# Gated attention/MLP mix: gate row turned by a matmul, b1 taken along in a projection unit, b2 loaded last, fusion chunks and attention sums regrouped

## Chip, cores, metric

One core of a Trainium2 chip. The metric is the device time of one execution in microseconds.

Names: PE is the matmul engine and PEld its weight loads, DVE the vector engine, ACT the scalar engine, POOL the GpSimd engine, SP the engine whose queue issues most DMAs. PSUM is the memory that PE writes to; a pair is two of its banks, and a unit can start only when its pair is free. A cast is a copy out of PSUM that also makes bf16 of it. K0, V2, Q1 and so on are units of the projections to keys, values and queries, numbered by pairs of token tiles. kv are the sums over the tokens, nm the numerators and den the denominators of the attention, hp the units of the first MLP layer.

## The reference, cut

```python
g = sigmoid((x * gate_w).sum(-1, keepdims=True))
a = A_ref(x, wqkv, w_phi, wo)      # linear attention, softmax feature maps, 16 heads of 28
b = gelu(x @ w1 + b1) @ w2 + b2    # F = 1792
return g * a + (1 - g) * b         # x: 2048 tokens of 448, bf16
```

The kernel fuses `wk @ w_phi` and `wq @ w_phi` on the chip first ("the fusions"). The gate sum `x @ gate_w` takes one more column: the gate row, turned to a column, is stored as column 448 of the fused weights, so that some projections are 449 wide and deliver it.

## The kernel before

The parts that the change and the argument touch:

```python
gb = consts.tile([32, P], BF16, name="gb")          # rows: 14 of b1, 4 of the gate
gbT = consts.tile([P, 32], BF16, name="gbT")        # the same, turned
...
nc.gpsimd.dma_start(gb[16:19, :], gate_w[0:384]...)
nc.gpsimd.dma_start(gb[19:20, :]..., gate_w[384:448]...)
nc.gpsimd.dma_start(gb[0:NJ, :], B_b1.rearrange("(j p) -> j p", p=P))
...
nc.gpsimd.dma_start(b2b[:], B_b2[None, :].to_broadcast([P, D]))   # about 11.4 us
load_wT(WkT, D)                       # turned loads, all on SP, in this order
load_wT(WqT, 0)
load_x(512, 512)
nc.sync.dma_start_transpose(gbT[:], gb[:])          # the gate turn
load_x(1024, 512)
...
def prep(W_T, W_out, s, copies):      # a fusion: chunks 2, 3, then 0, 1
    for h in (1, 0):
        w_ps = pair("w_ps", slot=(s + 1 - h) % 4)
        for i in range(2):
            c = 2 * h + i
            ... 4 matmuls ...
        copies[1 - h](out=W_out[:, 2*h:2*h+2, 0:D], in_=w_ps[:, :, 0:D])
...
twin(WkT)                             # ACT copy that chunk 3 of the fusion needs
prep(WkT, Wpk, 1, (nc.scalar.copy, nc.vector.tensor_copy))        # first fusion
...
prep(WqT, Wpq, 3, (nc.vector.tensor_copy, nc.vector.tensor_copy)) # second fusion
nc.vector.tensor_copy(out=Wpq[:, :, D], in_=gbT[:, 16:20])
nc.vector.tensor_copy(out=WvG[:, :, D], in_=gbT[:, 16:20])
nc.vector.tensor_copy(out=b1T[:], in_=gbT[:, 0:NJ])
...
visit([(K, 1), (V, 2)], [(Q, 0)], 0, 2)   # V2: first reader of the gate column of WvG
...
kv_half(0); kv_half(1)                # sums over the tokens, four head pairs each
... nm matmuls of four tiles, num_out (DVE) of four tiles, then hp units (w1) go on
```

The softmax here doesn't subtract the row's maximum and nothing guards it: scores larger than these inputs give would overflow.

## Time and profile before

| | |
|---|---|
| time | 152.51 us (median of 4) |
| span of the profiled run | 150.3 us |
| PE busy | 144.6 us, 96% |
| DVE, ACT, POOL busy | 54, 43, 49% |
| first matmul of the first fusion | 9.13 us |
| V2 begins | 16.03 us |
| first hp unit / first kv matmul | 43.44 / 61.57 us |
| last DVE operation begins | 147.22 us |

In the chain of waits and in the timelines a row is: start in us, duration in us, engine, source line, operation, output<-inputs; a bracket says how long the engine was idle before it and what ended that. A group of pipelined matmuls ("x6") is shown longer than the distance to the next one, because the ends are modelled; distances are taken from starts. Source lines shift between the kernels: w_ps is L315 before and L319 after, full projections are L204 and L203.

### The profile page before, as it was taken

The numbers are of one execution on the slowest core, as the hardware profiler recorded it, in microseconds if no ns is written. First come the engines' busy times: TensorE is split into PE (matmuls) and PEld (weight loads), VectorE is DVE, ScalarE is ACT, GpSimd is POOL, SyncE is SP. The second block draws the span as 40 slices with busy tenths as digits, with TensorE's granted clock in tenths as the row PEclk, the third lists the DMA queues.
The fourth block names the chain that finished last, engine by engine and source line by source line (L and its number), as shares of the span: only waits on it lengthen the run. The fifth ranks groups of instructions, "written<-read, shape, count | busy, mean of one in ns | idle before, by whom it ended". The sixth has DMA issues, their size and how long they took to land.

```text
span 150.3 us, 3083 instructions
## 1 busy us (share of the span) xinstructions
PE 144.6 (96%) x1281; PEld 74.2 (49%) x1281; DVE 81.7 (54%) x139; ACT 63.9 (43%) x71; POOL 73.4 (49%) x60
## 2 busy tenths in 40 slices
PE   7989799999999999999999999999999999999991
PEld 2445344555544444774444445554455555545561
DVE  0248488999969992049995000740637847044112
ACT  3346277989999876506767674000000000000000
POOL 7992127799996999900399960000611110024000
PEclk9999999999999999999999999999999999999999
DMA  4997969679999959994629991140302423303201
GB/s 88 290 196 120 209 153 191 136 170 220 218 219 231 361 126 138 212 120 96 74 41 173 173 139 36 37 100 10 122 31 65 100 70 70 70 2 120 65 31 31
DMA packets 46334, 18.99 MB, mean 126 GB/s; under 512 B 36784, under 2 KB 46128, under 8 KB 46320
## 3 DMA queue, kind: packets, MB, share of 16 engines
q1 hardware_dynamic: 45568, 18.18, 58.3%
q10 hardware_dynamic: 544, 0.37, 0.9%
q0 software_dynamic: 208, 0.23, 0.9%
q8 instruction: 10, 0.16, 0.5%
q14 instruction: 4, 0.03, 0.1%
HBM read 6.34 MB, written 1.84 MB: 54 GB/s over the span
## 4 chain that ended last, share of the span: by engine, by line
PE 88%; DMA 7%; SPq 1%; DVE 1%; issue 0%
PE hp L431 28%; PE y L526 28%; PE y L204 6%; PE q_ps L234 5%; DMA gel<-in_A_wqkv_dram 4%; PE k_ps L234 4%; DMA gbT<-gb 3%; PE v_ps L234 3%; PE nm L455 3%; PE kv L443 2%; PE v_ps L204 2%; PE q_ps L204 2%; PE k_ps L204 2%; PE y L214 1%; PE w_ps L315 1%; SPq L116 1%
## 5 line engine op out<-in xcount | busy, mean ns | idle before, releaser
L526 PE MATMUL y<-w_sb,gel 128*128 128x448 bf16 (+1 forms) x224 | 43.8, 350 | 0.0
L431 PE MATMUL hp<-xT,w_sb 64*128 64x512 bf16 x224 | 42.8, 376 | 0.0
L431 PE MATMUL hp<-xS,w_sb 64*128 64x512 bf16 x168 | 40.7, 376 | 0.0
L435 ACT ACTIVATE gel<-hp,b1T 128x1024 bf16<-128x1024 f32 x28 | 30.8, 1113 | 14.6 <-PE hp L431 14.2
L526 PEld LDWEIGHTS <-gel 128*128 128x128 bf16 x238 | 22.3, 98 | 19.3 <-issue 0.4
L431 PEld LDWEIGHTS <-w_sb 64*128 64x128 bf16 x392 | 18.9, 94 | 23.2 <-DVE o_all L468 0.5
L491 POOL TENSOR_SCALAR b2u<-b2b,ungate 128x448 f32<-128x448 bf16 x16 | 10.0, 637 | 40.5 <-DVE res L538 40.5
L261 POOL TENSOR_TENSOR gel<-gel,rec 128x1792 bf16<-128x1792 bf16 x8 | 25.6, 3212 | 7.1 <-DVE lg L270 4.8
L538 DVE SCALAR_TENSOR_TENSOR res<-y,ungate,b2u 128x448 bf16<-128x448 f32 (+1 forms) x16 | 10.3, 673 | 25.0 <-PE y L526 13.2
L261 POOL TENSOR_TENSOR phiq<-phiq,rec 128x1792 bf16<-128x1792 bf16 x4 | 12.7, 3211 | 9.6 <-DVE rec L260 9.6
L252 ACT ACTIVATE gel<-k_ps 128x896 bf16<-128x896 f32 x16 | 13.7, 922 | 6.5 <-PE k_ps L214 4.9
L258 DVE TENSOR_REDUCE sums<-gel 128x64 f32<-128x1792 bf16 x8 | 16.0, 1996 | 0.0
L462 DVE TENSOR_SCALAR den<-nm,enL 128x16 f32<-128x16 f32 x16 | 3.6, 228 | 17.2 <-PE nm L455 17.2
L261 POOL TENSOR_TENSOR phqT<-phqT,rec 128x1792 bf16<-128x1792 bf16 x4 | 12.7, 3213 | 0.0
L468 DVE TENSOR_TENSOR o_all<-nm,den 128x448 bf16<-128x448 f32 (+2 forms) x24 | 11.0, 485 | 0.6
L234 PEld LDWEIGHTS <-xT 64*128 64x128 bf16 x104 | 8.6, 94 | 4.8
L204 PEld LDWEIGHTS <-xT 128*128 128x128 bf16 x66 | 5.9, 98 | 8.1 <-issue 2.8
L280 DVE CAST vaug<-v_ps 128x896 bf16<-128x896 f32 x7 | 7.5, 1072 | 4.3 <-PE v_ps L214 2.9
L260 DVE RECIPROCAL rec<-sums 128x64 f32<-128x64 f32 x16 | 8.9, 553 | 1.1
L234 PEld LDWEIGHTS <-xS 64*128 64x128 bf16 x78 | 7.3, 94 | 3.6
L234 PE MATMUL q_ps<-gel,xT 64*128 64x448 bf16 x48 | 8.6, 349 | 0.0
L204 PE MATMUL y<-wo_sb,phiq 128*128 128x448 bf16 (+1 forms) x36 | 8.2, 349 | 0.0
(88 smaller groups left out, 149.5 us busy)
## 6 DMA issues: line engine op xcount, KB each, us to landing
w_sb<-in_B_w_dram SPq DMA_DIRECT2D x4, 784.0 KB, 12.3
out_dram<-res SPq DMA_DIRECT2D x15, 112.0 KB, 1.7
w_sb<-in_B_w_dram SPq DMA_DIRECT2D x1, 1568.0 KB, 16.6
xS<-xT SPq DMA_DIRECT2D x8, 96.0 KB, 2.2
phqT<-gel SPq DMA_DIRECT2D x4, 168.0 KB, 3.0
gel<-in_A_x_dram SPq DMA_DIRECT2D x2, 224.0 KB, 4.2
phqT<-gel SPq DMA_DIRECT2D x2, 168.4 KB, 3.2
gel<-in_A_wqkv_dram ACTq DMA_DIRECT2D x1, 336.0 KB, 4.3
```

The source lines that it names most:

```text
L204: nc.tensor.matmul(o, lhsT=self.L(i, slice(0, P), c), rhs=self.R(slice(0, P), c)[:, n0:n1], start=(first and c == 2), stop=(last and c == 1))
L234: nc.tensor.matmul(o, lhsT=tok, rhs=(W if direct else SWAPPED[name])[rows, c, 0:n], start=(k == 0), stop=own)
L252: nc.scalar.activation(out=o, in_=src, func=ACT.Exp, scale=(1.0, -1.0)[s])
L258: nc.vector.reduce_sum(out=sums[:], in_=ph, axis=AX.X)
L260: nc.vector.reciprocal(out=rec[:], in_=sums[:])
L261: eng.tensor_tensor(out=ph, in0=ph, in1=rec[:, :, :, None].to_broadcast([P, 32, 2, DH]), op=ALU.mult)
L431: nc.tensor.matmul(hp[:, i, :].rearrange("p (b t) -> p b t", b=2), lhsT=w1_sb[i * HP:(i + 1) * HP, k, j * P:(j + 1) * P], rhs=x_half(i, k, ...
L435: nc.scalar.activation(out=dst, in_=hp[:].rearrange("p i (b t) -> p i b t", b=2), func=ACT.Gelu_apprx_tanh, bias=b1T[:, j:j + 1])
L468: nc.vector.tensor_tensor(out=o_tok[:, col:col + (b - a) * DH].rearrange("p (q j d) -> p q j d", j=2, d=DH), in0=nm[:, a // 2:b // 2, 0:56 ...
L491: nc.gpsimd.tensor_scalar(out=b2u[t][:], in0=b2b[:], scalar1=ungate[:, place(t):place(t) + 1], scalar2=0.0, op0=ALU.mult, op1=ALU.add)
L526: nc.tensor.matmul(o, lhsT=gel[:, j, tok], rhs=w2_sb[:, j, n0:n1], start=(first and j == 0), stop=(last and j == NJ - 1))
L538: nc.vector.scalar_tensor_tensor(out=res[t][:, n0:n1], in0=o, scalar=ungate[:, e:e + 1], in1=b2u[t][:, n0:n1], op0=ALU.mult, op1=ALU.add)
```

## The change

The intent is to take the DMA turn of the gate row off the path to V2, to fill a hole in the fusions, to keep the b2 broadcast out of the crowded start, and to hide the second masking of the sums.

```diff
-    gb = consts.tile([32, P], BF16, name="gb")
-    gbT = consts.tile([P, 32], BF16, name="gbT")
+    gb = consts.tile([P, P], BF16, name="gb")
+    bb = consts.tile([P, P], BF16, name="bb")
...
-    nc.gpsimd.dma_start(gb[0:NJ, :], B_b1.rearrange("(j p) -> j p", p=P))
... (later on POOL, behind the phiq memset)
+    nc.gpsimd.dma_start(bb[0:NJ, :], B_b1.rearrange("(j p) -> j p", p=P))
...
-    nc.gpsimd.dma_start(b2b[:], B_b2[None, :].to_broadcast([P, D]))
... (last load on SP)
+    nc.sync.dma_start(b2b[:], B_b2[None, :].to_broadcast([P, D]))
...
-    nc.sync.dma_start_transpose(gbT[:], gb[:])
...
+    def turned_rows(cols, rows):
+        nc.tensor.matmul(cols, lhsT=rows[:], rhs=ident[:, 0:cols.shape[-1]], start=False, stop=True,
+                         skip_group_check=True)
... prep
+        for c in (2, 0, 3, 1):
+            ... 4 matmuls ...
+            if c == 3 and gates:
+                cols = w_ps[1][:, 1, D:D + 4]
+                turned_rows(cols, gb)
+                for W in (WvG, Wpq):
+                    nc.vector.tensor_copy(out=W[:, :, D], in_=cols)
         for h in (1, 0):
+            copies[1 - h](out=W_out[:, 2 * h:2 * h + 2, 0:D], in_=w_ps[h][:, :, 0:D])
...
-    prep(WqT, Wpq, 3, (nc.vector.tensor_copy, nc.vector.tensor_copy))
-    ... three copies from gbT ...
+    prep(WqT, Wpq, 3, (nc.vector.tensor_copy, nc.scalar.copy), True)
... in the unit V3
+    turned_rows(x_.un.ps[:, 1, 460:460 + NJ], bb)
+    nc.vector.tensor_copy(out=b1T[:], in_=t[:, 1, 460:460 + NJ])
... sums
-            kv_half(0)
-            kv_half(1)
+            parts = (range(0, 6), range(6, 8))
+            for qs in parts:
+                kv_part(qs)
```

More of the change, by code (lines that the diff above doesn't have):

```diff
@@ L113 @@
     nc.vector.memset(gb[:], 0.0)
+    nc.vector.memset(bb[:], 0.0)
     xv = x[0:512, :].rearrange("(j p) d -> p j d", p=P)
@@ L153 @@
                             compare_op=ALU.is_ge, fill=0.0, base=DH - 1, channel_multiplier=-1)
-    nc.gpsimd.dma_start(gb[16:19, :], gate_w[0:384].rearrange("(c p) -> c p", p=P))
-    nc.gpsimd.dma_start(gb[19:20, :].rearrange("o (i p) -> o i p", i=2),
+    nc.gpsimd.dma_start(gb[0:3, :], gate_w[0:384].rearrange("(c p) -> c p", p=P))
+    nc.gpsimd.dma_start(gb[3:4, :].rearrange("o (i p) -> o i p", i=2),
                         gate_w[None, None, 384:448].to_broadcast([1, 2, HP]))
-    nc.gpsimd.dma_start(gb[0:NJ, :], B_b1.rearrange("(j p) -> j p", p=P))
     pk4 = phik.rearrange("p t (q m) -> p (t q) m", m=HP)
@@ L283, in done @@
                 gate(u, t)
+            if u == 3:
+                nc.vector.tensor_copy(out=b1T[:], in_=t[:, 1, 460:460 + NJ])
     class K:
@@ L306, in twin, with prep @@
         nc.scalar.copy(out=W_T[:, :, D:512], in_=W_T[:, :, 384:D])
-    def prep(W_T, W_out, s, copies):
-        for h in (1, 0):
-            w_ps = pair("w_ps", slot=(s + 1 - h) % 4)
-            for i in range(2):
-                c = 2 * h + i
-                for m in range(4):
-                    n0, n1 = HEADS[m][0] * DH, HEADS[m][1] * DH
-                    nc.tensor.matmul(w_ps[:, i, n0:n1], lhsT=W_T[:, m, c * P:(c + 1) * P],
-                                     rhs=bd[:, m, 0:n1 - n0], start=(m == 0), stop=(m == 3),
-                                     skip_group_check=True)
-            copies[1 - h](out=W_out[:, 2 * h:2 * h + 2, 0:D], in_=w_ps[:, :, 0:D])
+    def turned_rows(cols, rows):
+        nc.tensor.matmul(cols, lhsT=rows[:], rhs=ident[:, 0:cols.shape[-1]], start=False, stop=True,
+                         skip_group_check=True)
+    def prep(W_T, W_out, s, copies, gates=False):
+        w_ps = [pair("w_ps", slot=(s + 1 - h) % 4) for h in (1, 0)][::-1]
+        for c in (2, 0, 3, 1):
+            h, i = c // 2, c % 2
+            for m in range(4):
+                n0, n1 = HEADS[m][0] * DH, HEADS[m][1] * DH
+                nc.tensor.matmul(w_ps[h][:, i, n0:n1], lhsT=W_T[:, m, c * P:(c + 1) * P],
+                                 rhs=bd[:, m, 0:n1 - n0], start=(m == 0), stop=(m == 3),
+                                 skip_group_check=True)
+            if c == 3 and gates:
[3 more added lines that the diff above has]
+                    nc.vector.tensor_copy(out=W[:, :, D], in_=cols)
+        for h in (1, 0):
+            copies[1 - h](out=W_out[:, 2 * h:2 * h + 2, 0:D], in_=w_ps[h][:, :, 0:D])
     def idle(n):
@@ L364 @@
     k0a.done()
-    prep(WqT, Wpq, 3, (nc.vector.tensor_copy, nc.vector.tensor_copy))
-    nc.vector.tensor_copy(out=Wpq[:, :, D], in_=gbT[:, 16:20])
-    nc.vector.tensor_copy(out=WvG[:, :, D], in_=gbT[:, 16:20])
-    nc.vector.tensor_copy(out=b1T[:], in_=gbT[:, 0:NJ])
+    prep(WqT, Wpq, 3, (nc.vector.tensor_copy, nc.scalar.copy), True)
     swap_w(WkS, Wpk, D)
@@ L392, in visit @@
             x_.un.fulls(True, False)
+            if kind is V and u == 3:
+                turned_rows(x_.un.ps[:, 1, 460:460 + NJ], bb)
             cl.append(x_)
@@ L436, in w1_unit, with kv_part @@
                              func=ACT.Gelu_apprx_tanh, bias=b1T[:, j:j + 1])
-    def kv_half(m):
+    def kv_part(qs):
         kv = pair("kv")[:, 0, :]
-        qs = range(4 * m, 4 * m + 4)
+        n = len(qs)
         for t in range(NT):
-            for q in qs:
-                nc.tensor.matmul(kv[:, (q % 4) * PW:(q % 4 + 1) * PW], lhsT=phik[:, t, q * P:(q + 1) * P],
-                                 rhs=vaug[:, t, q, :], start=(t == 0 and q == qs[0]),
+            for i, q in enumerate(qs):
+                nc.tensor.matmul(kv[:, i * PW:(i + 1) * PW], lhsT=phik[:, t, q * P:(q + 1) * P],
+                                 rhs=vaug[:, t, q, :], start=(t == 0 and i == 0),
                                  stop=(t == NT - 1), skip_group_check=True)
-        nc.vector.tensor_tensor(out=KVbd[:, 4 * m:4 * m + 4, :],
-                                in0=kv[:, 0:4 * PW].rearrange("p (q n) -> p q n", q=4),
-                                in1=mask[:, None, :].to_broadcast([P, 4, PW]), op=ALU.mult)
+        nc.vector.tensor_tensor(out=KVbd[:, qs[0]:qs[0] + n, :],
+                                in0=kv[:, 0:n * PW].rearrange("p (q n) -> p q n", q=n),
+                                in1=mask[:, None, :].to_broadcast([P, n, PW]), op=ALU.mult)
     def o_turned(t):
@@ L495 @@
         if j == 6:
-            kv_half(0)
-            kv_half(1)
+            parts = (range(0, 6), range(6, 8))
+            for qs in parts:
+                kv_part(qs)
             nms = [pair("nm"), pair("nm")]
             nms = [p[:, i, :] for p in nms for i in range(2)]
-            for m in range(2):
+            for qs in parts:
                 for t in range(4):
-                    num_mm(t, nms[t], range(4 * m, 4 * m + 4))
+                    num_mm(t, nms[t], qs)
             for t in range(4):
```

## The prediction

> **What bounds the kernel now.** I read the page first: PE is busy 96% of 150.3 us at a clock of 9 tenths or more in every slice, while DVE, ACT and POOL stand at 43 to 54%. So only time in which PE stands still, or PE work itself, can be won. Next I read the chain of waits that ended last, in order of time. It is PE almost throughout, and outside the start-up it leaves PE for long at one place only:
>
> ```profile
> 10.48 0.46 DVE gel L318
> 10.94 4.68 DMA gbT<-gb
> 15.61 0.02 issue
> 15.64 0.18 DVE gel L366
> 15.81 0.08 DVE gel L367
> 15.90 0.14 issue
> 16.03 1.30 PE v_ps L204 x6
> ```
>
> The columns are start, duration, what. The gate row is turned by a DMA transpose (issue at 10.94, landing at 15.61), two DVE copies put it into the weights, and unit V2, the first that reads the gate column of WvG, starts at 16.03.
>
> The third view is PE in time order from 9 to 18 us (start, duration, instruction, idle before it):
>
> ```profile
> 9.13 1.30 PE L315 MATMUL w_ps<-gel 128*128 128x140 bf16 x16 [0.33 <-DMA gel<-in_A_wqkv_dram]
> 10.37 0.55 PE L214 MATMUL v_ps<-gel,xT 64*128 64x448 bf16 x4
> ...
> 11.27 1.46 PE L204 MATMUL k_ps<-gel,xT 128*128 128x448 bf16 x6
> 12.56 1.09 PE L315 MATMUL w_ps<-gel 128*128 128x140 bf16 x16
> 13.49 1.30 PE L204 MATMUL k_ps<-gel,xT 128*128 128x448 bf16 x6
> 16.03 1.30 PE L204 MATMUL v_ps<-gel,xT 128*128 128x449 bf16 x6 [1.24 <-DVE gel L367]
> ```
>
> PE is idle 1.24 us before V2. Issue to issue the hole is longer: six K1 matmuls at about 0.19 us from 13.49 would let V2 issue at 14.63, so 1.40 us are lost. The weight loads in the same stretch show two smaller holes:
>
> ```profile
> 9.57 0.71 PEld L315 LDWEIGHTS <-gel 128*128 128x128 bf16 x12 [0.19 <-ACT gel L306]
> ...
> 11.62 0.66 PEld L204 LDWEIGHTS <-xT 128*128 128x128 bf16 x4 [0.24 <-issue]
> ```
>
> In the first fusion chunk 3 waits for the ACT copy of the doubled columns (9.11 to 9.51). In K0 the second matmul waits for the DVE copy of the fused half (10.48 to 11.57).
>
> The last place is around the attention sums, DVE and then weight loads:
>
> ```profile
> 65.36 0.40 DVE L446 TENSOR_TENSOR KVbd<-kv,mask 128x232 bf16<-128x232 f32 x1 [1.42 <-PE kv L443]
> 66.31 0.23 DVE L462 TENSOR_SCALAR den<-nm,enL 128x16 f32<-128x16 f32 x1 [0.55 <-PE nm L455]
> ```
>
> ```profile
> 71.06 0.98 PEld L431 LDWEIGHTS <-w_sb 64*128 64x128 bf16 x12 [0.49 <-DVE o_all L468]
> ```
>
> The second sum's masking (65.36 to 65.76) holds back half of the nm matmuls until 65.81, and the fourth hp unit after them waits for the PSUM pair that DVE empties at 71.00.
>
> **What the Trainium skill says.** (1) "VectorE: DVE Perf Modes", section "The three transpose paths", gives 390 ns for a 128x128 turn on TensorE and 1309 ns by the DMA crossbar. The order agrees; the size does not, for this trace's DMA turn of a 32x128 tile takes 4.68 us to landing. (2) The same page, section on the TRN2 errata, gives VectorE from PSUM 120 + FD cycles at 0.96 GHz. For 896 columns that is 1.06 us; the trace's casts take 1.09. (3) "TensorE: Matmul & The Clock Gate", section "Wait — 56ns, not 53.3ns?", says that start-to-start never falls below about 25 ns however small the matmul. The trace's kv matmuls of 58 columns run at 3.75 us / 128 = 29 ns with a full weight load each, so an extra 4 or 14 column matmul is about 0.03 us (estimate). (4) "PSUM — Partial Sum Buffer", section "The four PSUM rules": a matmul without the first flag overwrites columns whose bit an earlier first matmul cleared. That is why the turned rows may go into unused columns of an open bank; no run here shows it yet.
>
> **The change part by part.**
>
> *Gate row.* Removed: the DMA transpose and three DVE copies behind it. Added: one matmul of 4 columns (0.03 us) after the third chunk of the second fusion and two DVE copies of 128x4 from PSUM. The gate rows were requested at 3.34 and 3.88 and took 4.0 and 4.8 us to land, so 8.7 us; they are long there. What V2 then waits for is a new order on DVE: gate copies, then the cast of half 1, whose PSUM pair V2 takes. Without other shifts: 12 fusion matmuls at 0.93 us / 16 = 0.058 from 12.56 end issuing at 13.26, the gate matmul at 13.29. Before, the eighth matmul ended issuing at 13.02 and DVE began at 13.23, so 0.2 us later: 13.49. The DVE starts of small copies are 0.07 to 0.08 apart (15.64, 15.72, 15.79), so the cast runs from 13.64 to 14.73; DVE end to V2 was 0.14, so V2 at 14.87. That is 1.16 us earlier than 16.03. PE would be ready at 14.66, so about 0.2 us of waiting remains, on the cast. The cast of half 0 moves to ACT, which is idle 3.18 us after K0's exponentials: these end at 14.49, plus 0.91, so 15.4, ahead of Q0, its first reader, at about 16.5.
>
> *Chunks 2, 0, 3, 1.* In the first fusion chunk 0 fills the time that chunk 3 waited; by 9.61 the ACT copy (9.51) is done. Chunk 3 ends at the same time as before, so ACT's cast starts as before at 10.0; chunk 1 ends about 0.17 earlier, so DVE's cast ends at about 11.4 in place of 11.57. K0's second matmul, at about 11.62, can follow its first at 11.46, so the second fusion starts about 0.15 earlier (12.4). The ACT copy of v_ps that frees its slot ends at 11.72, and the DVE one for the other slot at about 12.4 against a use at 12.6. Everything of the paragraph above moves with it: V2 at about 14.72. The sum so far is 1.31 us.
>
> *b1 in V3.* One matmul of 14 columns on PE (0.03 us) and one DVE copy of 0.15 us, less than the 0.51 us that DVE idles in each of these visits. Cost 0.03 us on PE, and 0.03 for the gate matmul is already in the sum.
>
> *b2 on SP.* POOL loses 0.59 us of issuing at 11.42, where it then waited 0.91 us for the x load anyway. On SP it follows w2, whose landing was 38.55 + 16.6 = 55.2; its first reader is POOL after the last four norms, later than 85 us. Nothing in either direction.
>
> *Sums in six and two.* The same 128 kv matmuls. The first masking now lies beside 32 kv matmuls (0.93 us), the second, of 116 columns (about 0.28 us from the 0.40 of 232 columns), beside 24 nm matmuls at 0.028 = 0.68 us, so it is hidden. The last eight nm matmuls start at 65.16 + 0.68 = 65.84; the first pair is complete four later, so DVE starts at about 66.16 in place of 66.31. hp starts about 0.25 earlier, but its fourth unit waits for DVE's chain of four tiles, 4.7 us long and unchanged: what remains is 0.15 us.
>
> Sum: 1.31 - 0.03 + 0.15 = 1.43 us.
>
> **The SP queue.** The 1.12 us issue of the transpose goes, so all later SP issues can come about 1.3 earlier, the w1 loads among them. This matters: the earliest of four w1 loads landed 7.9 us after issue, their median is 12.3, so I estimate the second, which the first hp unit needs, at 41.9, only 1.2 us before PE wanted it at 43.09. Both ends move by about 1.3.
>
> **Rivals.**
> - *The x or w1 transfers take over the wait.* For it: that margin of 1.2 us, and DMA at 9 tenths in many slices. Against it: between 28.6 and 32.8 us the DMA share is 0.63, so the w1 loads start when SP issues them, and x of 512 to 1023 had landed by 12.91. If w1 stayed where it is, about 0.2 us would come back: 151.3.
> - *The DVE order keeps V2 late.* If PSUM-to-DVE latency or the two extra copies cost more, or the chunk order gives no start gain, V2 is at 14.9 to 15.2: gain 0.9 to 1.2, so 151.3 to 151.6.
> - *The start-up gain is absorbed by another engine in the projections (16 to 43 us).* DVE is busy 4.1 of 4.2 us there late on. But PE waits for nothing in these windows and every feeder starts earlier by the same amount, so I give this little: at worst 152.2.
> - *All holes close better than I think*, with hp's fourth unit not waiting at all: another 0.2 us, so 150.9.
>
> **Range and chances.** From the median 152.53, less 1.43, I say 151.1. The weak terms are V2's start (plus 0.3, minus 0.15) and the 0.15 at the sums, so 150.7 to 151.6. A gain over 2% needs 149.5, twice the holes listed; a loss over 2% needs 3 us of new wait on a path that has no candidate. Same within 2%: 0.98.
>
> **What would show it.** In the changed profile: no DMA in the chain between 10 and 16 us; the second fusion at about 12.4; V2 at about 14.7, its wait under 0.3 us and put down to DVE's cast of w_ps; Q0 without a wait on ACT; hp's first unit about 1.3 us earlier (about 41.95) with no DMA wait; the first den about 0.15 closer to the kv start, and nm as one run of 32 without a gap. A V2 start after 15.2, a weight load of hp waiting on the w1 transfer, or a new wait between 16 and 43 us would make the prediction wrong.

## The result, and the profile after

| | before | after |
|---|---|---|
| time, median of 4 | 152.51 us | 150.63 us (150.56 to 150.78) |
| profiled run: time / span | 152.35 / 150.3 | 150.57 / 148.5 |
| first fusion | 9.13 | 8.79 |
| second fusion | 12.56 | 12.10 |
| V2 | 16.03 | 14.40 |
| first hp unit (in the chain) | 43.44 | 41.82 |
| first kv matmul | 61.57 | 59.95 |
| fourth hp unit behind the sums | 71.06 | 69.28 |
| last DVE operation | 147.22 | 145.45 |

The ratio is 0.988, 95% interval 0.9863 to 0.9897. A ratio is the mean time of one kernel's fast runs over that of the other's of the same rounds, so it is not quite the ratio of the medians quoted. The time lies just below the predicted range of 150.7 to 151.6: the gain is 1.88 us by the medians and 1.78 in the two profiled runs, against 1.43 predicted.

The chain of waits of the changed kernel, for the stretch in which the gate turn stood before:

```profile
12.26 0.69 PE w_ps L319 x12
12.96 0.00 PE w_ps L310
12.96 0.25 PE w_ps L319 x4
13.21 1.14 PE k_ps L203 x6
14.35 0.05 issue
14.40 1.30 PE v_ps L203 x6
```

There is no DMA in it, and the new gate matmul (L310) takes no visible time. PE in time order, same kernel:

```profile
8.79 1.10 PE L319 MATMUL w_ps<-gel 128*128 128x140 bf16 x16
...
12.10 0.86 PE L319 MATMUL w_ps<-gel 128*128 128x140 bf16 x12
12.79 0.17 PE L310 MATMUL w_ps<-ident,gb 128*128 128x4 bf16 x1
12.82 0.39 PE L319 MATMUL w_ps<-gel 128*128 128x140 bf16 x4
13.05 1.30 PE L203 MATMUL k_ps<-gel,xT 128*128 128x448 bf16 x6
14.40 1.30 PE L203 MATMUL v_ps<-gel,xT 128*128 128x449 bf16 x6
```

From the gate matmul to the next one are 0.03 us, as estimated. Six K1 matmuls from 13.05 would let V2 issue at 14.19, so 0.21 us of the hole is left. What ends it? DVE, and then the weight loads:

```profile
13.03 0.24 DVE L326 CAST gel<-w_ps 128x4 bf16<-128x4 f32 x2 [1.01 <-PE w_ps L310]
13.17 1.08 DVE L328 CAST gel<-w_ps 128x896 bf16<-128x896 f32 x1
```

```profile
14.37 0.89 PEld L203 LDWEIGHTS <-xT 128*128 128x128 bf16 x6 [0.47 <-DMA xT<-in_A_x_dram]
```

The cast that frees V2's PSUM pair ends at 14.25; the profile, however, names the load of x, which landed just after it. This is the case in which the one that came last gets the whole wait. Which of the two counts is settled by other profiles below: it is the cast. The load came near, though. In all ten profiles of changed kernels it landed later than before: the POOL copy that waits for it starts at 13.68 to 14.36 us, against 12.70 to 13.26 in the six others. So the prediction's reading that this x "had landed by 12.91" did not carry over to the changed kernel; what delays the load was not tested.

Around the sums, DVE and then the weight loads:

```profile
63.68 0.28 DVE L456 TENSOR_TENSOR KVbd<-kv,mask 128x116 bf16<-128x116 f32 x1 [0.36 <-PE kv L453]
64.54 0.23 DVE L472 TENSOR_SCALAR den<-nm,enL 128x16 f32<-128x16 f32 x1 [0.58 <-PE nm L465]
```

```profile
63.45 0.97 PEld L465 LDWEIGHTS <-phqT 128*128 128x128 bf16 x32
64.47 4.21 PEld L441 LDWEIGHTS <-w_sb 64*128 64x128 bf16 x42
69.28 2.70 PEld L441 LDWEIGHTS <-w_sb 64*128 64x128 bf16 x28 [0.60 <-DVE o_all L478]
```

The second masking is 0.28 us long and hidden, the 32 nm weight loads run through in 0.97 us (1.17 before), and the fourth hp unit still waits for DVE.

**Where the time went.** V2 is 1.63 us earlier. This shift is carried without loss to the first kv matmul (1.62). At the fourth hp unit it is 1.78, at the last DVE operation 1.77. So the middle of the kernel took nothing back, and the sums gave 0.15. What differs from the prediction lies before V2: 1.63 in place of 1.31. And within it, from the first fusion to V2 the prediction had 14.72 - 9.13 = 5.59 us, and 14.40 - 8.79 = 5.61 was measured. The missing third of a microsecond is the start of the first fusion itself: 9.13 before, 8.79 after. The prediction had carried it over from one profile as if it were fixed. The ACT copy that doubles columns of the turned Wk starts when that load lands, and it shows the same shift, before and after:

```profile
9.11 0.40 ACT L306 COPY gel<-gel 128x256 bf16<-128x256 bf16 x1 [1.74 <-DMA gel<-in_A_wqkv_dram]
```

```profile
8.77 0.40 ACT L307 COPY gel<-gel 128x256 bf16<-128x256 bf16 x1 [1.33 <-DMA gel<-in_A_wqkv_dram]
```

SP issued the load at 2.94 in both kernels; from there to its landing were 6.1 us in the kernel before and 5.8 us in the changed one.

### The profile page after: what moved, and what is told of

The parts are those of the page before. It is cut to its first block, busy times and chain, and to the rows that moved or that the text cites. A ratio compares the mean times of both kernels' runs of the same rounds, so it can differ in the third digit from the quotient of the medians.

```text
span 148.5 us, 3085 instructions
## 1 busy us (share of the span) xinstructions
PE 144.0 (97%) x1283; PEld 74.1 (50%) x1283; DVE 80.7 (54%) x139; ACT 64.7 (44%) x72; POOL 72.9 (49%) x59
## 4 chain that ended last, share of the span: by engine, by line
PE 91%; DVE 3%; DMA 3%; ACT 1%; issue 0%
PE y L537 28%; PE hp L441 26%; PE y L203 6%; PE q_ps L233 5%; PE v_ps L203 4%; PE k_ps L233 4%; PE k_ps L203 3%; PE v_ps L233 3%; DMA gel<-in_A_x_dram 3%; PE kv L453 2%; PE nm L465 2%; DVE o_all L478 2%; PE q_ps L203 2%; PE w_ps L319 1%; PE y L213 1%; PE tp L343 1%
```

## The experiments

Theory at the start: the b1 load, which the change moves to later, had delayed the turned load of Wk that the first fusion reads. Rival: that load, and the one of x before it, land at another time in every run; the kernel before hid that behind the gate turn, and the changed one shows it. One further build (the second x load moved behind the first weight swap): a POOL copy then read x before its load; it was not run.

All profiles in one table. "Fusion" is the first matmul of the first fusion, "end" the start of the last DVE operation; all are read from the timelines and the chain, the two differences are worked out.

| profile | fusion | V2 | V2 - fusion | end | end - fusion |
|---|---|---|---|---|---|
| before | 9.13 | 16.03 | 6.90 | 147.22 | 138.09 |
| before_again | 8.76 | 15.70 | 6.94 | 146.89 | 138.13 |
| before_no_b1 | 8.85 | 15.91 | 7.06 | 147.09 | 138.24 |
| before_chunks | 8.62 | 16.01 | 7.39 | 147.19 | 138.57 |
| before_b2_sp | 8.97 | 15.35 | 6.38 | 146.53 | 137.56 |
| before_b2_sp_2 | 9.46 | 15.95 | 6.49 | 147.13 | 137.67 |
| after | 8.79 | 14.40 | 5.61 | 145.45 | 136.66 |
| after_again | 8.37 | 13.97 | 5.60 | 145.02 | 136.65 |
| after_third | 8.94 | 14.55 | 5.61 | 145.60 | 136.66 |
| after_b1_early | 8.87 | 14.47 | 5.60 | 145.52 | 136.65 |
| after_b2_pool | 8.98 | 14.59 | 5.61 | 145.64 | 136.66 |
| after_wk_first | 8.69 | 14.29 | 5.60 | 145.35 | 136.66 |
| after_sums_44 | 8.78 | 14.39 | 5.61 | 145.58 | 136.80 |
| after_nm_pairs | 9.09 | 14.69 | 5.60 | 145.66 | 136.57 |
| after_chunks_2301 | 8.70 | 14.21 | 5.51 | 145.26 | 136.56 |
| after_both_orders | 8.71 | 14.11 | 5.40 | 145.00 | 136.29 |

The last column repeats to 0.01 us in the six profiles whose chunk order, sums and nm order are the changed kernel's. It tells effects of 0.1 us apart that the times, which scatter by 0.2 to 1.0 us from run to run of one kernel, do not.

### after_again: the changed kernel once more

No edit.

> The changed kernel once more, unchanged, as the reference of this set. Both theories: 150.6 us, ratio about 0.988 to the kernel before. What is wanted is the scatter of one event: where the first fusion starts on PE, 9.13 us in the profile before and 8.79 in the profile after. Theory 'the early b1 load delayed the turned Wk load': 8.8 again. Rival 'the landing of that transfer scatters from run to run': anything between 8.8 and 9.2.

Measured: 150.44 us (150.12 to 150.68), ratio 0.9886 (0.9866 to 0.9906). The first fusion started at 8.37, 0.42 earlier than in the first profile of the same kernel and below the 8.8 of the theory and the 8.8 to 9.2 of the rival; everything after it came 0.43 earlier, to the last DVE operation. So the start scatters, and in the changed kernel that scatter goes straight through to the end.

### after_b1_early: the b1 load back in its old place

```diff
     nc.gpsimd.dma_start(gb[3:4, :]..., gate_w[384:448]...)
+    nc.gpsimd.dma_start(bb[0:NJ, :], B_b1.rearrange("(j p) -> j p", p=P))
```

> The changed kernel with the b1 load moved back to directly behind the two gate loads on POOL, as in the kernel before; all else as after. Theory 'the early b1 load cost 0.3 us at the first fusion': first fusion starts at 9.1, everything after it 0.3 later, time 150.9 to 151.0. Rival 'scatter, or some other part': first fusion at 8.8, time 150.6 as the changed kernel.

Measured: 150.64 us (150.62 to 150.8), ratio 0.9902 (0.9885 to 0.992). First fusion at 8.87, inside the 8.37 to 8.94 of the changed kernel itself. The theory asked for 9.1 and 150.9 or more. It falls, as a cost of 0.3 us; a tenth or two could not be told from the scatter.

### before_no_b1: the kernel before without its b1 load (bias zero on purpose)

```diff
-    nc.gpsimd.dma_start(gb[0:NJ, :], B_b1.rearrange("(j p) -> j p", p=P))
```

> The kernel before without its b1 load (the bias is then zero, a result that is wrong on purpose). Theory 'the early b1 load delays the turned Wk load': first fusion at 8.8 in place of 9.13, and 0.3 us faster than the kernel before where the DMA turn of the gate row does not take it back; as that turn is issued when the first x load has been issued and not by PE, I expect V2 to stay within 0.1 of 16.0 and the time at 152.4 to 152.5. Rival 'scatter': first fusion 8.8 to 9.2 without a pattern, same time.

Measured: 152.11 us (151.86 to 152.47), ratio 0.9998 (0.9981 to 1.0015). First fusion at 8.85, 0.28 earlier than in the profile before, but V2 only 0.12 earlier, and the time is the same. The run alone would fit both theories at the fusion; together with after_b1_early it fits the rival only.

### before_again: the kernel before, for its profile

No edit.

> The kernel before once more, for its profile. Theory 'the landing of the turned Wk load scatters, and the kernel before hides that scatter behind the DMA turn of the gate row': first fusion somewhere between 8.4 and 9.2, V2 nevertheless at 15.9 to 16.1, last DVE op at 147.1 to 147.3. Rival 'the kernel before has a later first fusion than the changed one': first fusion at 9.1 again.

Measured: one run, 152.0 us. First fusion at 8.76, so the rival "always 9.1" falls. V2 at 15.70 and the last DVE operation at 146.89, both 0.2 below what I expected: the gate turn was issued at 10.74 and landed after 4.5 us. Six K1 matmuls from 13.09 would have let V2 issue at 14.23, so the hole was 1.47 us here, against 1.40 in the profile that the prediction was made from.

### before_chunks: the chunk order alone

```diff
-        for h in (1, 0):
-            w_ps = pair("w_ps", slot=(s + 1 - h) % 4)
-            for i in range(2):
-                c = 2 * h + i
+        w_ps = [pair("w_ps", slot=(s + 1 - h) % 4) for h in (1, 0)][::-1]
+        for c in (2, 0, 3, 1):
+            h, i = c // 2, c % 2
```

> The kernel before with the fusion chunks in the order 2, 0, 3, 1 and nothing else changed. Theory 'V2 hangs on the DMA turn of the gate row and on nothing that PE does before it': second fusion 3.30 after the first in place of 3.43 (12.56 less 9.13), V2 nevertheless 4.8 to 5.1 after the issue of the turn, at 15.7 to 16.05, time 152.0 to 152.4, ratio 1.000. Rival 'the chunk order carries a part of the gain by itself': 0.13 faster or more and V2 below 15.6.

Measured: 152.45 us (152.3 to 152.68), ratio 0.9997 (0.9977 to 1.0016). PE in time order:

```profile
8.62 1.10 PE L314 MATMUL w_ps<-gel 128*128 128x140 bf16 x16
...
11.93 1.09 PE L314 MATMUL w_ps<-gel 128*128 128x140 bf16 x16
12.85 1.30 PE L204 MATMUL k_ps<-gel,xT 128*128 128x448 bf16 x6
16.01 1.30 PE L204 MATMUL v_ps<-gel,xT 128*128 128x449 bf16 x6 [1.86 <-DVE gel L367]
```

The second fusion is 3.31 after the first, as expected. K1 starts 0.64 us earlier than in the profile before (0.51 of it the earlier first fusion of this run), and V2 is 0.02 earlier: all of it went into a longer wait for the gate copies. (V2 was 5.25 behind the issue of the turn at 10.76, a little more than the 5.1 I had given.) This shows the structure of the kernel before: V2 is the later of two chains, one over Wk, PE and DVE that scatters, and one over the gate turn that did not care about it.

### before_b2_sp and before_b2_sp_2: the place of b2 alone

```diff
-    nc.gpsimd.dma_start(b2b[:], B_b2[None, :].to_broadcast([P, D]))
     nc.sync.dma_start(w2_sb[:], B_w2.rearrange("(j p) n -> p j n", p=P))
+    nc.sync.dma_start(b2b[:], B_b2[None, :].to_broadcast([P, D]))
```

> The kernel before with the b2 broadcast as the last load on SP. Prediction's step: nothing in either direction; last DVE op at 146.9 to 147.3, V2 4.8 to 5.1 after the issue of the gate turn. Rival 'the b2 broadcast at 11.4 us slows the gate turn on the DMA engines': the turn takes less than 4.4 from issue to landing (4.68 in the profile before) and V2 comes before 15.6.

Measured: one run, 151.59 us. This was a surprise. The gate turn's time from issue to landing, in the kernel before and then in this one, from the views of the tile gbT:

```profile
L179 SPq DMA_TRANSPOSE gbT<-gb x1: 1118/1118/1118, 10.9 to 10.9; - x1
DMA to landing us min/median/max: 4.7/4.7/4.7
```

```profile
L178 SPq DMA_TRANSPOSE gbT<-gb x1: 1118/1118/1118, 11.1 to 11.1; - x1
DMA to landing us min/median/max: 2.3/2.3/2.3
```

The first number triple is the issue in ns, 1118 in both; only the landing differs. It was 4.7, 4.5, 4.4 and 4.8 us in the four profiles in which POOL issues the b2 broadcast at 10.9 to 11.4 us, and 2.3 without it. Since one look is one look, the kernel was run again, with rounds:

> The kernel before with the b2 broadcast as the last load on SP, a second time and timed: in the first look the gate turn took 2.3 us to land in place of 4.4 to 4.8, and V2 came at 15.35. Theory 'the b2 broadcast, in flight at the same time, stretches the turn by 2 us; without it V2 waits for the gate copies behind two casts on DVE': turn 2.2 to 2.6 us again, V2 6.3 to 6.5 after the first fusion (15.35 less 8.97 was 6.38), so 15.0 to 15.5, time 0.5 to 0.7 below the kernel before, ratio 0.995 to 0.997. Rival 'a single lucky transfer': turn 4.4 to 4.8, V2 at 15.7 to 16.05, ratio 1.000.

Measured: 151.72 us (151.56 to 152.2), ratio 0.9967 (0.995 to 0.9985). The turn landed in 2.3 us again, and DVE made the gate copies directly behind its casts:

```profile
13.56 2.09 DVE L317 CAST gel<-w_ps 128x896 bf16<-128x896 f32 x2 [0.67 <-PE w_ps L314]
15.56 0.17 DVE L365 COPY gel<-gbT 128x4 bf16<-128x4 bf16 x1
```

V2 was 6.49 behind the first fusion, in the expected band; V2's absolute time (15.95) is above the expected 15.5 only because this profile has the latest first fusion of all, 9.46. So the b2 part, which the prediction had called nothing, is worth about 0.5 us (0.0033 of 152.4; by the interval 0.2 to 0.8) in the kernel before. The Trainium skill's page "DMA: Bandwidth & Descriptors", section "Queues, rings and completion order", says that each DMA engine takes packets from the queues that have work in turn; that a transfer on POOL's queue can stretch one on SP's fits it, but why a broadcast of 112 KB costs a turn of 8 KB two microseconds is not shown by these runs.

### after_b2_pool: b2 back on POOL in the changed kernel

```diff
+    nc.gpsimd.dma_start(b2b[:], B_b2[None, :].to_broadcast([P, D]))      # behind the mask copy
...
-    nc.sync.dma_start(b2b[:], B_b2[None, :].to_broadcast([P, D]))
```

> The changed kernel with the b2 broadcast back on POOL at about 11.4 us, as in the kernel before. Theory 'b2 mattered only through the gate turn, which is gone': V2 5.60 after the first fusion, last DVE op 136.65 after it, time as the changed kernel, ratio 0.987 to 0.989. Rival 'the broadcast now stretches the x load of 512 to 1023 that V2 reads, which lands at 13.7 to 14.4 against a V2 at 14.0 to 14.7': x lands later than the cast of w_ps ends plus 0.1, V2 5.7 to 6.5 after the first fusion, 0.2 to 0.9 slower.

Measured: 150.7 us (150.48 to 151.26), ratio 0.9904 (0.9884 to 0.9923), just outside the expected 0.987 to 0.989 with an interval that covers it. V2 5.61 behind the first fusion, end 136.66 behind it: exactly as with b2 on SP. Once the gate turn is gone, b2's place does not count. Two parts of the change thus pay for the same wait: either shortens it, and the matmul removes it.

### after_chunks_2301: the chunks in the old order in the changed kernel

```diff
-        for c in (2, 0, 3, 1):
+        for c in (2, 3, 0, 1):
```

> The changed kernel with the fusion chunks in the old order 2, 3, 0, 1 (the gate matmul then comes after the second chunk). Prediction's step: the hole behind chunk 2 in the first fusion is back, so the second fusion starts about 3.43 after the first in place of 3.30; in the second fusion the gate matmul and the cast of half 1 come one chunk (0.23) earlier, so that V2 is bound by PE itself and not by the cast: first fusion to V2 about 5.5 to 5.65, against 5.60. So about no difference in the end. Rival 'the order is worth the 0.15 that I gave it': 5.75.

Measured: one run, 150.4 us. PE in time order:

```profile
12.13 0.63 PE L319 MATMUL w_ps<-gel 128*128 128x140 bf16 x8
12.59 0.17 PE L310 MATMUL w_ps<-ident,gb 128*128 128x4 bf16 x1
12.62 0.62 PE L319 MATMUL w_ps<-gel 128*128 128x140 bf16 x8
13.08 1.30 PE L203 MATMUL k_ps<-gel,xT 128*128 128x448 bf16 x6
14.21 1.30 PE L203 MATMUL v_ps<-gel,xT 128*128 128x449 bf16 x6
```

The second fusion is 3.43 behind the first (8.70), 0.13 more than the 3.30 of the prediction, as expected. But the gate matmul and with it the cast come one chunk earlier, and V2 follows K1 without a wait: 5.51 behind the first fusion in place of 5.60. The order 2, 0, 3, 1 therefore costs 0.09 us in the changed kernel. My 0.15 for it was wrong, in sign too.

### after_sums_44: the sums in four and four

```diff
-            parts = (range(0, 6), range(6, 8))
+            parts = (range(0, 4), range(4, 8))
```

> The changed kernel with the sums in parts of four and four, as before. Prediction's step: from the first kv matmul to the fourth hp unit behind the sums 0.15 longer than in the changed kernel (9.33 from 59.95 to 69.28), so about 9.48, with the last DVE op 136.80 after the first fusion in place of 136.65. Rival 'the parts are worth nothing': 9.33 and 136.65.

Measured: one run, 150.69 us. Fourth hp unit at 69.42, first kv matmul at 59.94, so 9.48; end 136.80 behind the first fusion. Both to the hundredth: six and two is worth 0.15 us.

### after_nm_pairs: the nm matmuls pair by pair

```diff
-            for qs in parts:
-                for t in range(4):
-                    num_mm(t, nms[t], qs)
+            for ts in ((0, 1), (2, 3)):
+                for qs in parts:
+                    for t in ts:
+                        num_mm(t, nms[t], qs)
```

> The changed kernel with the nm matmuls in another order: tiles 0 and 1 with both parts, then tiles 2 and 3. Theory 'hp's fourth unit waits for DVE's chain of four tiles, which starts when the first PSUM pair is complete': the pair is complete after 16 nm matmuls in place of 28, so the first den starts about 0.3 earlier against the start of nm (0.6 after it in place of 0.9), the wait of the fourth hp unit on DVE falls from about 0.2 us to nothing, time about 150.4. Rival 'the fourth unit waits for something else, or the second masking is not ready for the earlier use': no change, 150.6.

Measured: 150.59 us (150.34 to 150.79), ratio 0.9895 (0.9876 to 0.9914). Half a hit. The first den came 0.91 behind the first nm matmul (64.69 - 63.78) in place of 1.06, not the 0.6 I expected, and the end is 0.08 earlier. The rest is the rival's: the second masking ended at 64.26, PE wanted it earlier, and the nm matmuls took 1.18 us to the first hp unit (64.96 - 63.78) in place of 0.99.

### after_wk_first: the turned Wk load issued earlier

```diff
-    nc.sync.dma_start(wphi[:, 0:3, :], ...)
-    nc.sync.dma_start(wphi[0:HP, 3, :], ...)
+    nc.scalar.dma_start(wphi[:, 0:3, :], ...)
+    nc.scalar.dma_start(wphi[0:HP, 3, :], ...)
```

> The changed kernel with the two small w_phi loads issued from ACT in place of SP, so that SP issues the turned Wk load 1.1 us earlier (1.83 in place of 2.94). Theory 'after the change the end hangs on the first fusion, which hangs on this load': first fusion at about 8.4, where PE is ready for it, in every run; V2 5.60 later at 14.0; last DVE op at about 145.0; time 150.1 to 150.2 with less scatter than the changed kernel. Rival 'the landing is set by the load on the DMA engines, not by its issue, or the x load that PE needs first is pushed back': first fusion at 8.8 or later, time 150.5 or more.

Measured: 150.5 us (150.43 to 150.75), ratio 0.99 (0.9875 to 0.9926). The rival is nearer: first fusion at 8.69, and Wk, issued 1.11 us earlier, landed at 8.66, against 8.24 to 8.92 in the three profiles of the changed kernel (starts of its ACT copy). So the earlier issue did not bring it earlier. PE runs into the fusion without a pause, but only just, for the weight load of the fusion still waited for Wk. PE, and then that weight load:

```profile
4.55 1.03 PE L343 MATMUL tp<-ident,gel 128*128 128x128 bf16 x8
...
6.86 1.99 PE L203 MATMUL v_ps<-gel,xT 128*128 128x448 bf16 x9
```

```profile
8.68 0.94 PEld L319 LDWEIGHTS <-gel 128*128 128x128 bf16 x16 [0.27 <-DMA gel<-in_A_wqkv_dram]
```

PE began with x at 4.55; in after_again, where PE too ran straight into the fusion at 8.37, it began at 4.21. From there to the fusion are 4.14 and 4.16 us. So the fusion starts at the later of two times, the landing of Wk and PE's own arrival, and both scatter. In twelve of the sixteen profiles, this one included, it starts 0.02 or 0.03 us after the landing of Wk (the start of the ACT copy). In the other four (after_again, before_again, before_b2_sp, after_nm_pairs) PE arrives later. PE's arrival hangs on the first x load, but also on PE itself: in after_again x had landed by 4.13, and the chain of waits begins with PE's warm-up matmuls; in before_again, before_b2_sp and after_nm_pairs the three V matmuls after the first turns took 0.96 to 1.09 us to the next instruction in place of 0.57 to 0.66 (starts of the PE timelines). Why they did was not looked for. Taking Wk out of the start was not achieved here, so what that would gain stays open.

### after_both_orders: what the experiments point to

```diff
-        for c in (2, 0, 3, 1):
+        for c in (2, 3, 0, 1) if gates else (2, 0, 3, 1):
...
-            for qs in parts:
-                for t in range(4):
-                    num_mm(t, nms[t], qs)
+            six, two = parts
+            for t, qs in ((0, six), (1, six), (2, six), (0, two), (1, two), (3, six), (2, two), (3, two)):
+                num_mm(t, nms[t], qs)
```

> The changed kernel with the first fusion in the order 2, 0, 3, 1 and the second in 2, 3, 0, 1, and the nm matmuls in the order: six of tiles 0, 1, 2, two of 0 and 1, six of 3, two of 2 and 3. Theory: the first fusion to V2 is 3.30 + 2.08 = 5.38 in place of 5.60; the first den comes 0.82 after the first nm in place of 1.06, and hp's fourth unit waits 0.03 in place of 0.27; last DVE op 136.2 after the first fusion in place of 136.65, so time 150.0 to 150.1. Rival 'another wait takes over in the one place or the other': 136.4 or more, 150.3.

Measured: 150.12 us (149.7 to 150.35), ratio 0.9841 (0.9818 to 0.9864), with a right output. V2 5.40 behind the first fusion (5.38 expected), the first den 0.91 behind the first nm (0.82 expected), the end 136.29 behind the first fusion (136.2 expected, 136.4 by the rival), 0.37 less than the changed kernel. The fourth hp unit still waits 0.11 or so:

```profile
64.20 4.21 PEld L441 LDWEIGHTS <-w_sb 64*128 64x128 bf16 x42
68.84 3.13 PEld L441 LDWEIGHTS <-w_sb 64*128 64x128 bf16 x32 [0.43 <-DVE o_all L478]
```

(4.64 us from the first hp load to the fourth unit's, against 69.28 - 64.47 = 4.81 in the changed kernel.) By its chain this version beats both kernels; the intervals of the timed ratios, 0.9818 to 0.9864 and 0.9859 to 0.9895 for after_third beside it, overlap by a hair.

### after_third: the changed kernel beside it

No edit.

> The changed kernel a third time, on the same chip as the run before it. Last DVE op 136.65 after the first fusion whatever the start of that fusion (8.4 to 9.1), V2 5.60 after it, time 150.4 to 150.6, ratio to the kernel before 0.987 to 0.990.

Measured: 150.65 us (150.54 to 150.73), ratio 0.9877 (0.9859 to 0.9895). First fusion 8.94, V2 5.61 and end 136.66 behind it, as expected; the time is 0.05 above the expected band.

## Why the prediction was wrong, and where it was right

- **What bounds the kernel** was read rightly: the only long wait on the path was the gate turn, and removing it is most of the gain.
- **From the first fusion to V2**: 5.59 predicted, 5.60 or 5.61 measured in the eight profiles whose chunks and gate copies are the changed kernel's. Gate matmul 0.03, 0.2 from PE to DVE, two short copies, the cast, all as worked out. The remaining wait is the cast's, as said: in after_again, after_third, after_b1_early and after_nm_pairs the x load had landed (its POOL copy had begun) 0.3 to 0.7 us before V2, and V2 kept its 5.60. So the x load that the first profile after names did not set V2's time there either, for V2 came 5.61 behind the fusion as in the others.
- **The step that failed** is "the second fusion starts about 0.15 earlier (12.4)" with "V2 at about 14.72": it took the start of the first fusion, 9.13, from the profile before and held it fixed. The mechanism was right; this term was mis-sized. That start is 8.37 to 9.46 in the sixteen profiles, and 8.79 in the profile after, which is 0.34 us; the missing gain was 0.35 between the two profiled runs, and the other terms of the sum, V2 behind the fusion taken as one, are off by 0.02 or less. In the kernel before it did not matter, because V2 hung on the other chain: with fusions from 8.62 to 9.13 V2 was at 15.70 to 16.03, in no relation. How much of this was luck? If V2 had come 5.60 behind the fusion of the same run, the four profiles with the turn and the early broadcast (before, before_again, before_no_b1, before_chunks) would give a gain at V2 of 1.30, 1.34, 1.46 and 1.79 us. So the profile that the prediction was made from gave the least of the four, before_again alone would hardly have mended it, and the profile after then drew an earlier fusion. With means (V2 15.91 in those four, the fusion 8.79 in the ten changed kernels) the gain is 1.52 at V2 and, with 0.15 at the sums less 0.01 for b1, 1.66 in all (an estimate), against 1.81 to 1.88 by the medians of the three timings; the rest is within their intervals and is not explained. What a removed wait is worth is the distance to the *usual* end of the chain that takes over, not to its end in the one profile. The range gave V2 only 0.15 downwards.
- **Is the early start a gift of the change?** The mean of the first fusion is 8.97 in the six kernels built on the one before and 8.79 in the ten built on the changed one, with ranges 8.62 to 9.46 and 8.37 to 9.09. The b1 load, the first suspect, was excluded as a cost of 0.3 us. A small shift by another part is neither shown nor excluded; why these two loads scatter stays open.
- **The chunk order** was credited with 0.15 us. It moves the second fusion by that (3.31 in place of 3.43) and loses it again, since its gate matmul comes a chunk later: -0.09 net. The sum survived only because the step before it already assumed the later place. The prediction's own reading that V2 waits for the cast should have told it.
- **b2: "nothing in either direction"** holds for the changed kernel (136.66 with either place) and not for the kernel before, where b2 alone gives about 0.5 us. I had the sign of it in hand: a turn of a 32x128 tile took 4.68 us where the page "VectorE: DVE Perf Modes" of the Trainium skill, section "The three transpose paths", gives 1.3 for a 128x128 one, and I noted the difference without asking what else was in flight. (Undisturbed the turn takes 2.3, so the broadcast was a part of that difference and not all of it.)
- **b1 in V3**: 0.03 predicted; from V2 to the first hp unit are 27.41 us before and 27.42 after, so 0.01.
- **Sums**: 0.15 predicted, 0.15 measured, with its mechanism (masking 0.28 us, hidden; fourth unit still waiting).
- **SP queue and w1**: both ends moved alike, no wait of hp on a DMA, as said; the rival of a w1 wait did not come, while that of the x load came near (see the profile after).
- **Turned rows in unused PSUM columns**, which no run had shown: every changed kernel passed the comparison. For b1 this says little, as the kernel without b1 passed too; how much an error in the gate would show was not tested.

## What to carry to other kernels

A wait in one profile is the distance between two chains, and the hidden one may have been late in that run: before sizing a removal, take several profiles and look how the chain that will take over scatters. Differences between events of one trace (here: end less first fusion) repeat to 0.01 us where whole times scatter by half a microsecond, so small parts of a change are better judged by them. And a transfer that takes much longer than expected (4.4 to 4.8 us here, 2.3 when left alone) deserves a look at what else is in flight, before a new path is built around it.

## What the Trainium skill lacked or had wrong

- "VectorE: DVE Perf Modes", section "The three transpose paths": 1309 ns for a 128x128 turn by the DMA crossbar, without saying from where to where it counts. Here a 32x128 turn takes 2.3 us from issue to landing undisturbed (two profiles) and 4.4 to 4.8 us beside a broadcast on POOL's queue (four profiles).
- "DMA: Bandwidth & Descriptors" has no figure for what a broadcast load does to a small transfer beside it: 2.1 to 2.5 us here, by those same numbers.
- No page says how much the landing of a kernel's first loads scatters from run to run: in three profiles of the changed kernel the first x load by 0.4 us (the weight loads that wait for it start at 4.57, 4.13 and 4.35), the turned weight load by 0.7 us (8.77, 8.24 and 8.92, the starts of the ACT copy that waits for it).
